# Four more layers of the first block in three passes, and the second block's attention jobs cut in steps behind each layer's gate

## The chip, the core and the metric

One core of a Trainium2 chip. Five engines run side by side and meet only at semaphores: TensorE (PE, with its weight loads PEld), VectorE (DVE), ScalarE (ACT), GpSimd (POOL) and SyncE (SP), whose queue issues all the DMAs here. Each works through its own instructions in the order in which they stand, so an instruction that waits holds everything behind it on that engine. The metric is the time of one execution on the device, in microseconds; less is better.

## What is computed

An attention with decay (a linear recurrence over 768 steps) for 4 sequences and 8 heads of 48, followed by two feed-forward parts on the 3072 tokens of width 384.

```python
for t in range(S):                                   # attention, S = 768
    cur = np.einsum('bhd,bhe->bhde', u[None] * kt, vt)
    y[:, :, t] = np.einsum('bhd,bhde->bhe', rt, state + cur)
    state = wt[:, :, :, None] * state + np.einsum('bhd,bhe->bhde', kt, vt)
...
h = x @ w_in                                         # first part, 384 -> 2048 -> 384
g = h * np.clip(h + 3.0, 0.0, 6.0) / 6.0
x = g @ w_out
...
xn = x / rms * rms_g                                 # second part, 384 -> 1536 -> 384
gate = xn @ w_gate
out = (gate * sigmoid(gate) * (xn @ w_val)) @ w_out
```

## The kernel before

**Blocks, layers, turns.** The tokens go in six blocks of 512 (a chunk of 128 steps of each of the four sequences). For each block the first feed-forward part runs over 16 layers f of 128 hidden columns: `ff1` multiplies the block by the layer's `w_in` into a PSUM tile `hps` (two buffers), ScalarE and VectorE make the gate of it (`emit_act`: a ReLU of `hps` on ScalarE, L455, then a VectorE instruction that takes the minimum and multiplies by `hps`, L456), and `ff2` multiplies the result by the layer's `w_out` into three accumulators `o`. `ff2` of a layer runs two turns after its `ff1`. In the first block the first five layers are taken in two halves of 256 tokens, so that block has 21 turns (0 to 9 are halves; from turn 10 on, turn n is layer n - 5); each later block has 16. Turn 21 is the first of the second block.

**Two ways to multiply.** A layer is done in fp32 (L444, L450: three instructions for `ff1`, three for `ff2`, each of which the profile records as two), or in three fp32r passes of a high part and a low part of both operands (L438, L467: nine instructions each). In the first block the layers below `F32_F` = 12 go in fp32, the four others and all later blocks in three passes. The passes need both operands split. For the weights, `Weight.parts` copies the high part on ScalarE (L161) and subtracts on VectorE (L162). For the block's input, `x_parts` does so for three slices (L594, L595). For the gate's output, `emit_split` copies on ScalarE (L460) and subtracts on GpSimd (L461). Weights come as 64-bit words; `Weight.scale` (ScalarE, L146) and `Weight.bits` (VectorE, L151 and L152) make fp32 of them, and a DMA then writes them to the place where `parts` later reads them.

**Attention jobs.** Each block has four jobs, one for each sequence; jobs 4 to 7 make the second block's input during turns 6 to 20 of the first block, and start at turns n = 6, 9, 12 and 15. A job consists of

- `scans`: two VectorE scans (L273, 128x520) with a reciprocal between them (L281); `bonus1` on GpSimd (L300, L301);
- `muls`: two VectorE multiplications by the scans' results (L296), then `bonus2`, a reduction (L305), and `decay` on GpSimd;
- `fill`: eight ScalarE activations into a tile `a` (L331), which need the reduction's result;
- `pe_a` (L350) and `pe_kt` (L338) on TensorE, which read what `muls` wrote; `choose`: two predicated copies on VectorE into `a` (L356);
- `pe_y` (L386, L392) and `pe_u` (L365) on TensorE, which read `a`; `copy_y` and eight DMAs; then `split` (L414 on ScalarE, L415 on GpSimd) into `xt`, the next block's input.

**What sets the order.** Three lists for each turn n are run around the layer's work: `before[n]`, then `ff1` with its gate, then `between[n]`, then `ff2` of the layer of turn n - 2, then `behind[n]`. `pin` makes the order in which the code emits binding on every engine.

Of the kernel before, what the change touches and what calls it, by code (L numbers as in the profile page):

```python
# [9 lines left out]
F32 = mybir.dt.float32  # L10
# [3 lines left out]
AF = mybir.ActivationFunctionType  # L14
ALU = mybir.AluOpType
AX = mybir.AxisListType

B, H, S, D = 4, 8, 768, 48
# [5 lines left out]
KT = DM // 128  # L24
F1 = 2048 // 128
# [4 lines left out]
WP = 4 * DM  # L30
NG = F2 // 3
LAGS = (5, 0, 0, 0, 0, 0)
F32_F = 12


@with_exitstack
def kernel(
# [15 lines left out]
    nc = tc.nc  # L53
# [23 lines left out]
    x0 = st_p.tile([128, KT, TOK], F32, tag="x0", name="x0", bufs=1)  # L77
# [53 lines left out]

    class Weight:
        def __init__(self, src):
            self.src, self.near = src, False

        def load(self):
            self.raw = st_p.tile([128, 2 * DM], U64, tag="raw", name="raw", bufs=3)
# [11 lines left out]
        def bits(self):  # L149
            x = st_p.tile([128, 2 * DM], U32, tag="x", name="x", bufs=3)  # L150
            nc.vector.tensor_scalar(x, self.words()[0], 29, None, ALU.logical_shift_right)  # L151
            nc.vector.scalar_tensor_tensor(  # L152
                out=x, in0=self.mag.bitcast(U32), scalar=3, in1=x, op0=ALU.logical_shift_left, op1=ALU.bitwise_or)
            self.x = x.bitcast(F32).rearrange("p (a n) -> p a n", a=2)
            nc.sync.dma_start(
                out=self.dst[:, :, 1, :].bitcast(U32), in_=x.rearrange("p (a n) -> p a n", a=2))
            if not self.near:
                self.x = self.dst[:, :, 1, :].bitcast(F32)

        def parts(self):  # L160
            nc.scalar.activation(out=self.dst[:, :, 0, :], in_=self.x, func=AF.Copy)  # L161
            nc.vector.tensor_tensor(  # L162
                out=self.dst[:, :, 1, :], in0=self.x, in1=self.dst[:, :, 0, :].bitcast(F32), op=ALU.subtract)


# [89 lines left out]
    xts = {0: xt_p.tile([128, KT, 2, TOK], F32R, tag="xt", name="xt")}  # L255

    class Job:
# [16 lines left out]
                out=x, data0=x, data1=dd.rearrange("p a h j -> p (a h j)"),  # L274
                initial=0.0, op0=ALU.mult, op1=ALU.add)

        def scans(self):
            nc.vector.memset(dd[:, :, :, 0:1], 1.0)
            self.scan(0)
            self.s1, self.s2 = self.w[:, 0], self.w[:, 1]  # L280
            nc.vector.reciprocal(out=dd[:, :, :, 0:1], in_=self.s1[:, :, :, HF:HF + 1])  # L281
            self.scan(1)

        def decay(self):
            b = self.b
# [172 lines left out]
    def emit_split(a, n, p=None):  # L458
        g = (p or rg_p).tile([128, 2, n], F32R, tag="g", name="g")
        nc.scalar.activation(out=g[:, 0, :], in_=a, func=AF.Copy)  # L460
        nc.gpsimd.tensor_tensor(out=g[:, 1, :], in0=a, in1=g[:, 0, :].bitcast(F32), op=ALU.subtract)  # L461
        return g
# [62 lines left out]
    wa = [Weight(wa_d[f]) for f in range(F1)]  # L525
# [9 lines left out]
    before, between, behind = ([[] for _ in steps] for _ in range(3))  # L535

    def plan(j, n):

        jb = jobs[j]
        before[n] += [jb.scans, jb.bonus1]  # L540
        before[n + 1] += [jb.muls, jb.bonus2, jb.decay]
        before[n + 2] += [jb.fill]
        between[n + 2] += [jb.pe_a, jb.pe_kt, jb.choose, jb.copy_kt]
        between[n + 3] += [jb.pe_y, jb.pe_u, jb.copy_y, jb.add_u]
        if j + 2 < len(jobs):
            behind[n + 3] += [lambda: jobs[j + 2].load("w", "rk", "v")]
        if j + 1 < len(jobs):
            behind[n + 1] += [lambda: jobs[j + 1].load("rks")]
        before[n + 5] += [jb.split]


    j0, j1, j2, j3 = jobs[:B]
# [22 lines left out]
        if f + 3 < F1:  # L575
            behind[n] += [wa[f + 3].load]
    for f in range(F1):
        before[f + 19 if f < F32_F else f + LAGS[0] - 1] += [wa[f].parts]
    behind[2] += [lambda: jobs[4].load("w", "rk", "rks", "v")]
    behind[4] += [lambda: jobs[5].load("w", "rk", "v")]  # L580

# [6 lines left out]
    for c in range(1, NC_):  # L588
        norm_plan(c, first[c], False)

    def x_parts():
        for k in range(KT):
            h = xts[0][:, k, 0, :]
            nc.scalar.activation(out=h, in_=x0[:, k, :], func=AF.Copy)  # L594
            nc.vector.tensor_tensor(out=xts[0][:, k, 1, :], in0=x0[:, k, :], in1=h.bitcast(F32), op=ALU.subtract)  # L595

    behind[F32_F + LAGS[0] - 2] += [x_parts]
    acc, norms, todo = None, {}, []


# [12 lines left out]
    def ff1(c, f, cols):  # L613
        n = cols.stop - cols.start
        ps = ps_h.tile([128, n], F32, tag="h", name="hps")
        if c == 0 and f < F32_F:
            if cols.start:
# [4 lines left out]
        else:  # L622
# [3 lines left out]
            g = emit_split(a, n)  # L626
        x = wa[f].x[:, 1] if c == 0 and f < F32_F else wpair[f][:, 1]
        todo.append((c, f, cols, g, x))

    def ff2(c, f, cols, g, x):  # L630
        nonlocal acc
        first, last = f == 0 and cols.start == 0, f == F1 - 1
        if first:
            acc = new_acc()
        if c == 0 and f < F32_F:
            emit_out_f32(acc, x, g, first, cols)
# [5 lines left out]
    def run(fs):  # L642
        for x in fs:
            x()
# [294 lines left out]
    for i in range(2):  # L939
        nc.sync.dma_start(  # L940
            out=uc[64 * i:64 * i + D, :, i], in_=u_d.rearrange("o (p i d) -> i d (o p)", p=NP, i=2)[i])
# [178 lines left out]
    for j in range(6 * NG + 1):  # L1120
        p, k = divmod(j, 2 * NG)
# [32 lines left out]
        want, n = {4: 7, 5: 7, 6: 6}.get(j, 9), 0  # L1154
# [107 lines left out]
```

## Time and profile before

| | |
|---|---|
| median of 3 runs | 950.96 us (950.94 to 951.01) |
| the profiled execution | 955.21 us, of which its span 953.4 us |
| PE busy | 932.8 us (98%) |
| DVE, POOL, ACT busy | 638.9, 540.5, 476.3 us |
| granted PE clock | 0.996 (mean), of full speed |
| PE share of the chain that ended last | 88% |

The rows below are from the profiled execution, whose times count from the span's start. A busy PE is an engine with instructions under way; the length of a group is best read in the chain of work that ended last, where a group starts when the one before it has ended.

### The profile page before, as it was taken

What the parts mean: (1) busy time and instruction counts of PE and PEld (TensorE: products, weight loads), DVE (VectorE), ACT (ScalarE), POOL (GpSimd) and SP (SyncE); (2) the same over time, 40 slices, a digit from 0 to 9 for tenths busy, and PEclk for the clock granted to TensorE, in tenths of its full rate; (3) what the DMA queues carried; (4) which work ended last, traced back from release to release, by engine and by line L of the source; (5) the groups of instructions that cost most, each with busy time, mean ns of one, the idle gap of its engine ahead of it and who ended that gap; (6) DMA issues with size and microseconds to landing.
All of it is one profiled execution on the core that took longest, in us unless ns stands there. A gap on an engine that the chain in (4) does not pass through costs nothing.

```text
span 953.4 us, 14292 instructions
## 1 busy us (share of the span) xinstructions
PE 932.8 (98%) x5085; PEld 736.3 (77%) x5085; DVE 638.9 (67%) x908; ACT 476.3 (50%) x946; POOL 540.5 (57%) x459
## 2 busy tenths in 40 slices
PE   5899999999999999999999999999999999999998
PEld 5775577778878887777888888787777887888876
DVE  7667776878768787857555386557798557554543
ACT  4544656645654654564454554446545444433331
POOL 0033345766856676774465677579466679235425
PEclk9899999999999999999999999999999999999999
DMA  9686742236654563661662477854699642744321
GB/s 342 237 320 224 279 148 81 84 111 219 208 179 164 174 200 125 219 208 39 236 220 72 152 290 263 290 210 177 203 375 324 260 180 83 248 166 147 151 78 67
DMA packets 63127, 184.77 MB, mean 194 GB/s; under 512 B 8912, under 2 KB 23248, under 8 KB 58448
## 3 DMA queue, kind: packets, MB, share of 16 engines
q1 hardware_dynamic: 63056, 183.87, 54.5%
q8 instruction: 40, 0.66, 0.3%
q14 instruction: 31, 0.25, 0.1%
HBM read 134.29 MB, written 39.32 MB: 182 GB/s over the span
## 4 chain that ended last, share of the span: by engine, by line
PE 88%; DVE 4%; DMA 3%; issue 2%; ACT 2%; POOL 1%; SPq 1%; POOLq 0%; ACTq 0%; DVEq 0%
PE o L467 17%; PE hps L438 16%; PE o L744 14%; PE pe L744 10%; PE pc L744 8%; PE pa L744 4%; PE hps L444 3%; PE o L450 3%; PE pb L744 3%; PE aps L350 2%; PE yps L392 2%; DMA w<-in_dram 2%; PE pd L744 1%; PE ktp L338 1%; PE yps L386 1%
## 5 line engine op out<-in xcount | busy, mean ns | idle before, releaser
L461 POOL TENSOR_TENSOR g<-a,g 128x512 fp32r<-128x512 f32 x84 | 116.5, 1386 | 139.0 <-ACT g L460 138.4
L467 PE MATMUL o<-g,wide_b 128*128 128x512 f32 x441 | 113.4, 399 | 0.0
L456 DVE SCALAR_TENSOR_TENSOR a<-a,hps 128x512 f32<-128x512 f32 x84 | 57.3, 682 | 82.9 <-ACT a L455 82.5
L438 PE MATMUL hps<-xt,wide_b 128*128 128x512 f32 x441 | 111.9, 398 | 0.0
L744 PE MATMUL o<-xt,wide_b 128*128 128x512 f32 x405 | 107.6, 395 | 0.0
L438 PEld LDWEIGHTS hps<-xt,wide_b 128*128 128x128 f32 x441 | 82.7, 187 | 21.2 <-issue 1.0
L455 ACT ACTIVATE a<-hps,half 128x512 f32<-128x512 f32 x84 | 57.3, 682 | 81.0 <-PE hps L438 75.6
L467 PEld LDWEIGHTS o<-g,wide_b 128*128 128x128 f32 x441 | 81.2, 188 | 19.5 <-issue 0.5
L460 ACT ACTIVATE g<-a 128x512 fp32r<-128x512 f32 x84 | 53.1, 633 | 82.3 <-DVE a L456 80.5
L744 PEld LDWEIGHTS o<-xt,wide_b 128*128 128x128 f32 x405 | 75.9, 188 | 18.5 <-ACT planes L234 0.4
L467 PE MATMUL o<-g,wide_a 128*128 128x512 f32 x315 | 78.7, 394 | 0.0
L438 PE MATMUL hps<-xt,wide_a 128*128 128x512 f32 x315 | 77.6, 390 | 0.2 <-POOL xt L415 0.2
L273 DVE TENSOR_TENSOR_SCAN w<-w,dd 128x520 f32<-128x520 f32 x48 | 73.4, 1529 | 4.7 <-DMA w<-in_dram 3.1
L438 PEld LDWEIGHTS hps<-xt,wide_a 128*128 128x128 f32 x315 | 59.0, 188 | 13.3 <-POOL xt L415 0.6
L467 PEld LDWEIGHTS o<-g,wide_a 128*128 128x128 f32 x315 | 58.2, 188 | 12.3 <-issue 0.2
L779 DVE TENSOR_TENSOR q<-pc,q 128x512 f32<-128x512 f32 x80 | 55.0, 688 | 17.8 <-PE pc L744 7.0
L844 POOL TENSOR_TENSOR q<-q,q 128x512 f32<-128x512 f32 x40 | 55.1, 1378 | 14.5 <-DVE q L779 14.3
L331 ACT ACTIVATE a<-iperm,cb 128x128 f32<-128x128 f32 x192 | 58.5, 389 | 0.1
L744 PE MATMUL o<-g,wide_b 128*128 128x512 f32 (+1 forms) x216 | 55.4, 390 | 0.0
L300 POOL TENSOR_TENSOR rks<-rks 128x384 f32<-128x384 f32 x20 | 30.4, 1522 | 43.4 <-DMA rks<-in_dram 38.1
L841 ACT ACTIVATE q<-q 128x512 f32<-128x512 f32 x40 | 25.3, 632 | 51.3 <-DVE q L779 51.3
L844 POOL TENSOR_TENSOR o<-o,o 128x512 f32<-128x512 f32 x10 | 14.1, 1406 | 63.4 <-DVE o L779 63.4
(204 smaller groups left out, 2019.8 us busy)
## 6 DMA issues: line engine op xcount, KB each, us to landing
wraw<-in_dram SPq DMA_DIRECT2D x36, 384.0 KB, 4.1
wide_b<-wo SPq DMA_DIRECT2D x12, 1152.0 KB, 8.0
w<-wd SPq DMA_DIRECT2D x10, 1280.0 KB, 6.0
wide_b<-wd SPq DMA_DIRECT2D x10, 1280.0 KB, 6.0
w<-in_dram SPq DMA_DIRECT2D x24, 520.0 KB, 3.8
rk<-in_dram SPq DMA_DIRECT2D x24, 512.0 KB, 5.0
raw<-in_dram SPq DMA_DIRECT2D x16, 768.0 KB, 7.7
rks<-in_dram SPq DMA_DIRECT2D x20, 384.0 KB, 5.0
```

Source lines behind the costliest of these rows:

```text
L273: nc.vector.tensor_tensor_scan(out=x, data0=x, data1=dd.rearrange("p a h j -> p (a h j)"), initial=0.0, op0=ALU.mult, op1=ALU.add)
L300: nc.gpsimd.tensor_tensor(out=x, in0=x, in1=self.rks[:, 1, :], op=ALU.mult)
L331: nc.scalar.activation(out=self.head(h), in_=iperm, func=AF.Copy, scale=self.cb[:, h, :])
L438: nc.tensor.matmul(ps, slot[:, l, k * 128:(k + 1) * 128], xt[:, k, r, :], start=(k == 0 and j == 0), stop=(k == KT - 1 and j == 2))
L455: nc.scalar.activation(out=a, in_=ps, func=AF.Relu, scale=1.0 / 6.0, bias=half)
L456: nc.vector.scalar_tensor_tensor(out=a, in0=a, scalar=1.0, in1=ps, op0=ALU.min, op1=ALU.mult)
L460: nc.scalar.activation(out=g[:, 0, :], in_=a, func=AF.Copy)
L461: nc.gpsimd.tensor_tensor(out=g[:, 1, :], in0=a, in1=g[:, 0, :].bitcast(F32), op=ALU.subtract)
L467: nc.tensor.matmul(acc[m][:, cols], slot[:, l, m * 128:(m + 1) * 128], g[:, r, :], start=(first and j == 0), stop=(parts or last and j == ...
L744: nc.tensor.matmul(ps, lhs[:, l, :], rhs[:, r, :], start=first and j == 0, stop=True, skip_group_check=not (first and j == 0))
L779: nc.vector.tensor_tensor(out=out, in0=a, in1=b, op=op)
L844: eng.tensor_tensor(out=o, in0=src, in1=self.gate.o[i], op=ALU.mult)
```

## The change

`F32_F` goes from 12 to 8: layers 8 to 11 of the first block now also go in three passes. Their weights' `parts` move from turns 27 to 30 to turns 12 to 15. Weights of layers 8 to 15 are split from the tile in which `bits` made them (`stays`), without the DMA to their place and back. `x_parts` stood whole behind turn 15; it now takes a slice in each of turns 8, 9 and 10, with its subtraction on GpSimd in place of VectorE (`LOW_POOL` is empty: weights are still subtracted on VectorE).

In jobs 4 to 7 the steps stand elsewhere: the first scan behind the gate of turn n, the second behind the gate of turn n + 1, `muls` and `bonus2` behind that (before, both scans stood ahead of the gate of turn n, and `muls` ahead of the gate of turn n + 1), `fill` behind the gate of turn n + 2 in place of ahead of it. `split` of the first three jobs of every block stands behind its turn in place of ahead of it.

```diff
-F32_F = 12
+F32_F = 8
+LOW_POOL = ()
...
             self.x = x.bitcast(F32).rearrange("p (a n) -> p a n", a=2)
+            if self.stays:
+                return
             nc.sync.dma_start(
...
-        def parts(self):
+        def parts(self, pool=False):
             nc.scalar.activation(out=self.dst[:, :, 0, :], in_=self.x, func=AF.Copy)
-            nc.vector.tensor_tensor(
+            (nc.gpsimd if pool else nc.vector).tensor_tensor(
                 out=self.dst[:, :, 1, :], in0=self.x, in1=self.dst[:, :, 0, :].bitcast(F32), op=ALU.subtract)
...
-        def scans(self):
+        def scan_a(self):
             nc.vector.memset(dd[:, :, :, 0:1], 1.0)
             self.scan(0)
             self.s1, self.s2 = self.w[:, 0], self.w[:, 1]
+
+        def scan_b(self):
             nc.vector.reciprocal(out=dd[:, :, :, 0:1], in_=self.s1[:, :, :, HF:HF + 1])
             self.scan(1)
...
         jb = jobs[j]
-        before[n] += [jb.scans, jb.bonus1]
-        before[n + 1] += [jb.muls, jb.bonus2, jb.decay]
-        before[n + 2] += [jb.fill]
-        between[n + 2] += [jb.pe_a, jb.pe_kt, jb.choose, jb.copy_kt]
+        if jb.c == 1:
+            between[n] += [jb.scan_a, jb.bonus1]
+            between[n + 1] += [jb.scan_b, jb.decay]
+            behind[n + 1] += [jb.muls, jb.bonus2]
+            between[n + 2] += [jb.fill, jb.pe_a, jb.pe_kt, jb.copy_kt]
+            behind[n + 2] += [jb.choose]
+        else:
+            before[n] += [jb.scans, jb.bonus1]
+            before[n + 1] += [jb.muls, jb.bonus2, jb.decay]
+            before[n + 2] += [jb.fill]
+            between[n + 2] += [jb.pe_a, jb.pe_kt, jb.choose, jb.copy_kt]
         between[n + 3] += [jb.pe_y, jb.pe_u, jb.copy_y, jb.add_u]
...
-        before[n + 5] += [jb.split]
+        (before if jb.b == B - 1 else behind)[n + 5] += [jb.split]
...
-        before[f + 19 if f < F32_F else f + LAGS[0] - 1] += [wa[f].parts]
+        if f < F32_F:
+            before[f + 19] += [wa[f].parts]
+        else:
+            before[f + LAGS[0] - 1].insert(0, lambda f=f: wa[f].parts(f in LOW_POOL))
...
-    def x_parts():
-        for k in range(KT):
...
+    def x_parts(k):
+        h = xts[0][:, k, 0, :]
+        nc.scalar.activation(out=h, in_=x0[:, k, :], func=AF.Copy)
+        nc.gpsimd.tensor_tensor(out=xts[0][:, k, 1, :], in0=x0[:, k, :], in1=h.bitcast(F32), op=ALU.subtract)
+
+    for k in range(KT):
+        behind[F32_F + LAGS[0] - 5 + k] += [lambda k=k: x_parts(k)]
...
+    for f in range(F32_F, F1):
+        wa[f].stays = True
```

**VectorE around the gates of turns 13 and 14** (job 6, n = 12; a gate is the instruction that reads `hps`; `dd` and `w` are the scans' tiles, `x` the weights being made, `wide_b` their parts). Before, from the first scan's setup, over the gate of turn 12 (the L456 in the middle), to the gate of turn 13:

```order
L278 MEMSET dd 128x8
L273 SCALAR_TENSOR_TENSOR w<-w,dd 128x520
L281 RECIPROCAL dd<-w 128x8
L273 SCALAR_TENSOR_TENSOR w<-w,dd 128x520
L456 SCALAR_TENSOR_TENSOR g<-g,hps 128x512
L374 TENSOR_TENSOR st_105<-st_105,ups 128x192
L151 TENSOR_SCALAR x<-raw 128x768
L152 SCALAR_TENSOR_TENSOR x<-mag,x 128x768
L296 TENSOR_TENSOR rk<-rk,w 128x8x64 x2
L305 TENSOR_REDUCE cb<-rks 128x8
L456 SCALAR_TENSOR_TENSOR g<-g,hps 128x512
```

In the kernel now, from the gate of turn 13 to `choose` behind the gate of turn 14:

```order
L465 SCALAR_TENSOR_TENSOR a<-a,hps 128x512
L286 RECIPROCAL dd<-w 128x8
L276 SCALAR_TENSOR_TENSOR w<-w,dd 128x520
L305 TENSOR_TENSOR rk<-rk,w 128x8x64 x2
L314 TENSOR_REDUCE cb<-rks 128x8
L152 TENSOR_SCALAR x<-raw 128x768
L153 SCALAR_TENSOR_TENSOR x<-mag,x 128x768
L165 TENSOR_TENSOR wide_b<-x,wide_b 128x2x384
L465 SCALAR_TENSOR_TENSOR a<-a,hps 128x512
L365 COPY_PREDICATED a<-mask,aps 128x512 x2
```

The second scan stood ahead of the gate of turn 12 and the two multiplications ahead of that of turn 13; now all three stand behind the gate of turn 13, and the weights' subtraction of layer 10 (L165) stands between them and the gate of turn 14.

**ScalarE at turn 14** (`a<-iperm` is `fill`, L340 now and L331 before; `g<-hps` and `a<-hps` are the ReLU, `g<-a` the copy of the gate's output). Before:

```order
L455 ACTIVATE g<-hps,half 128x512
L146 ACTIVATE mag<-raw 128x768
L414 ACTIVATE xt<-x 128x3x128
L331 ACTIVATE a<-iperm,cb 128x128 x8
L455 ACTIVATE g<-hps,half 128x512
L343 ACTIVATE kt<-ktp 128x512
```

Now:

```order
L464 ACTIVATE a<-hps,half 128x512
L469 ACTIVATE g<-a 128x512
L340 ACTIVATE a<-iperm,cb 128x128 x8
L352 ACTIVATE kt<-ktp 128x512
L423 ACTIVATE xt<-x 128x3x128
L164 ACTIVATE wide_b<-x 128x2x384
```

`fill` stood ahead of the turn's ReLU, and now stands behind the ReLU and behind the copy of the gate's output, which waits for VectorE.

**VectorE from the gate of turn 18 to that of turn 19.** Before:

```order
L456 SCALAR_TENSOR_TENSOR a<-a,hps 128x512
L374 TENSOR_TENSOR st_107<-st_107,ups 128x192
L278 MEMSET dd 128x8
L273 SCALAR_TENSOR_TENSOR w<-w,dd 128x520
L281 RECIPROCAL dd<-w 128x8
L273 SCALAR_TENSOR_TENSOR w<-w,dd 128x520
L162 TENSOR_TENSOR wide_a<-wide_a 128x2x384
L162 TENSOR_TENSOR wide_b<-wide_b 128x2x384
L456 SCALAR_TENSOR_TENSOR a<-a,hps 128x512
```

Now:

```order
L465 SCALAR_TENSOR_TENSOR a<-a,hps 128x512
L383 TENSOR_TENSOR st_107<-st_107,ups 128x192
L165 TENSOR_TENSOR wide_b<-x,wide_b 128x2x384
L281 MEMSET dd 128x8
L276 SCALAR_TENSOR_TENSOR w<-w,dd 128x520
L286 RECIPROCAL dd<-w 128x8
L276 SCALAR_TENSOR_TENSOR w<-w,dd 128x520
L165 TENSOR_TENSOR wide_a<-wide_a 128x2x384
L465 SCALAR_TENSOR_TENSOR a<-a,hps 128x512
```

The weights' subtraction of layer 15, which stood behind the scans of the next job, now stands ahead of them.

## Rows read from the trace of the kernel before

**Rows 1.** Part 1 of the page: busy us, share of the span, instructions.
```profile
PE 932.8 (98%) x5085; PEld 736.3 (77%) x5085; DVE 638.9 (67%) x908; ACT 476.3 (50%) x946; POOL 540.5 (57%) x459
```

**Rows 2.** Stretches of the first block: us, then each engine's busy us, clock, DMA share, GB/s.
```profile
core 0: us, PE busy (x) PEld busy (x) DVE busy (x) ACT busy (x) POOL busy (x), PEclk, DMA share, GB/s
58.00:87.00 29.00, 29.00 (x228) 20.90 (x228) 19.85 (x33) 15.57 (x34) 7.16 (x8) 1.00 0.74 261
87.00:115.00 28.00, 28.00 (x129) 14.33 (x128) 20.55 (x32) 15.13 (x33) 10.07 (x11) 1.00 0.71 244
```

**Rows 3.** Waits of PE from 60 to 260 us: total us, times, longest us.
```profile
PE yps L386 <- DVE a L356: 1.2, 2, 0.7
PE hps L438 <- POOL xt L415: 0.2, 1, 0.2
```

**Rows 4.** Chain that ended last, 64 to 142 us: start us, us, what.
```profile
64.11 1.09 PE aps L350 x16
...
75.81 2.58 PE hps L444 x6
...
91.36 2.58 PE o L450 x6
...
113.33 2.09 PE hps L438 x9
...
115.42 1.09 PE aps L350 x16
...
139.26 2.11 PE o L467 x9
```

**Rows 5.** VectorE in order of time: start us, us, engine, line, operation, tiles, count, [idle before].
```profile
62.06 0.42 DVE L456 SCALAR_TENSOR_TENSOR g<-g,hps 128x256 f32<-128x256 f32 x1 [1.30 <-ACT g L455]
...
70.02 0.21 DVE L281 RECIPROCAL dd<-w 128x8 f32<-128x8 f32 x1
70.26 1.24 DVE L273 TENSOR_TENSOR_SCAN w<-w,dd 128x520 f32<-128x520 f32 x1
...
71.99 1.29 DVE L296 TENSOR_TENSOR rk<-rk,w 128x512 f32<-128x512 f32 x2
73.20 0.55 DVE L305 TENSOR_REDUCE cb<-rks 128x8 f32<-128x384 f32 x1
75.27 0.69 DVE L456 SCALAR_TENSOR_TENSOR g<-g,hps 128x512 f32<-128x512 f32 x1 [1.53 <-ACT g L455]
75.88 0.55 DVE L151 TENSOR_SCALAR x<-raw 128x768 uint32<-128x768 uint32 x1
76.46 0.96 DVE L152 SCALAR_TENSOR_TENSOR x<-mag,x 128x768 uint32<-128x768 uint32 x1
...
92.11 0.69 DVE L456 SCALAR_TENSOR_TENSOR g<-g,hps 128x512 f32<-128x512 f32 x1 [0.16 <-ACT g L455]
...
115.80 0.96 DVE L162 TENSOR_TENSOR wide_b<-wide_b 128x768 fp32r<-128x768 f32 x1 [2.13 <-ACT wide_b L161]
...
117.27 1.34 DVE L356 COPY_PREDICATED a<-mask,aps 128x512 f32<-128x512 uint32 x2
```

**Rows 6.** ScalarE in order of time, same columns.
```profile
112.60 2.44 ACT L331 ACTIVATE a<-iperm,cb 128x128 f32<-128x128 f32 x8
...
117.39 0.63 ACT L460 ACTIVATE g<-a 128x512 fp32r<-128x512 f32 x1 [1.05 <-DVE a L456]
...
125.00 0.83 ACT L161 ACTIVATE wide_b<-wide_b 128x768 fp32r<-128x768 f32 x1
```

**Rows 7.** GpSimd in order of time, same columns.
```profile
132.07 1.62 POOL L461 TENSOR_TENSOR g<-a,g 128x512 fp32r<-128x512 f32 x1 [3.02 <-ACT g L460]
133.65 1.74 POOL L415 TENSOR_TENSOR xt<-x,xt 128x384 fp32r<-128x384 f32 x1
...
190.49 1.95 POOL L300 TENSOR_TENSOR rks<-rks 128x384 f32<-128x384 f32 x1
```

**Rows 8.** VectorE in order of time while GpSimd works beside it, same columns.
```profile
189.71 1.91 DVE L273 TENSOR_TENSOR_SCAN w<-w,dd 128x520 f32<-128x520 f32 x1
...
195.69 2.42 DVE L296 TENSOR_TENSOR rk<-rk,w 128x512 f32<-128x512 f32 x2
```

More of the change, by code (lines that the diff above doesn't have):

```diff
@@ L133, in __init__ @@
         def __init__(self, src):
-            self.src, self.near = src, False
+            self.src, self.near, self.stays = src, False, False
         def load(self):
@@ L280, in scans @@
             self.s1, self.s2 = self.w[:, 0], self.w[:, 1]
+        def scan_b(self):
             nc.vector.reciprocal(out=dd[:, :, :, 0:1], in_=self.s1[:, :, :, HF:HF + 1])
             self.scan(1)
+        def scans(self):
+            self.scan_a()
+            self.scan_b()
         def decay(self):
@@ L589 @@
         norm_plan(c, first[c], False)
-    def x_parts():
-        for k in range(KT):
[L593 to L597, printed above, removed]
+    def x_parts(k):
[4 more added lines that the diff above has]
+        behind[F32_F + LAGS[0] - 5 + k] += [lambda k=k: x_parts(k)]
     acc, norms, todo = None, {}, []
```

## Prediction

> **What bounds the kernel now.** I read part 1 of the page first: PE is busy for 932.8 of 953.4 us [rows 1]. Then the stretches of the first block in which the change works: from 58 to 115 us PE is busy without a gap, at the full granted clock, while VectorE works 19.9 of 29 and 20.6 of 28 us [rows 2]. Then the waits of PE: from 60 to 260 us it waited 1.2 us in two places for `choose` (DVE `a`, L356) and 0.2 us for the second block's input (POOL `xt`, L415), and for nothing else [rows 3]. So here the sum of TensorE's own groups is the time. A change can gain by making them shorter, and can win back 1.4 us of waits at most; moving work between the other engines gains nothing more, and loses as soon as TensorE has to wait. Since TensorE works in order, a wait of `pe_a` or `pe_y` also holds the `ff2` and the `ff1` behind it. That is what I look for.
>
> **What the shorter groups give.** A whole layer's `ff1` takes 2.58 us in fp32 and 2.09 in three passes; `ff2` takes 2.58 and 2.11 [rows 4]. Four layers: 4 x (0.49 + 0.47) = 3.8 us. The weights' subtractions of layers 8 to 11 leave turns 27 to 30, where VectorE also serves jobs; the shorter of the two waits for `choose` (1.2 - 0.7 = 0.5 us, rows 3) stands there, in turn 30, and I count it as gone. Gain: 4.3 us.
>
> The page "FP8 and Floating Point Precision" of the Trainium skill (TensorE Precision Notes) has fp32 as four passes through the array, by which three passes would cost three quarters. The rows give 0.81, not 0.75. By the page a group would save 0.64 us, the change 5.1 us in place of 3.8, and the forecast would be 1.3 us lower; the rows decide.
>
> **Edits at no cost.** `x_parts` on GpSimd, 7.2 and 10.1 us busy in stretches of 29 and 28 [rows 2], is wanted at turn 13 and made by turn 10; if it were late, turn 13 would wait for what is left of three subtractions. Eight DMAs of weights leave SP's queue, which brings the loads behind them forward; PE waits for no DMA here [rows 3]. The copies and subtractions for layers 8 to 11 and their gate outputs lie on ScalarE and GpSimd, which have room; on VectorE 0.96 us a turn is added [rows 5], which counts in the next part. `split` of three jobs in four moves past one turn's work, with the last job still ahead of it; only the last one is on the edge.
>
> **What the moved steps cost.** Before, both scans and `muls` of a job were done ahead of the gate of turn n + 1. Now the second scan starts behind that gate, and `pe_a` in turn n + 2 needs `muls`. Behind the gate stand the reciprocal, 0.21 us, the scan, 1.24, and `muls`, 1.29 [rows 5]: 2.7 us. With GpSimd at work beside it a scan took 1.91 us and `muls` 2.42 [rows 8], so the same three take up to 4.5. I set that against what TensorE has to do meanwhile.
>
> Job 4 (turns 7 and 8, halves): the gate of turn 7 ends at 62.06 + 0.42 = 62.48 [rows 5], so `muls` end at 65.2; TensorE reaches `pe_a` at 64.11 [rows 4]. It waits 1.1 us. Little stands on GpSimd there, so I take no contention.
>
> Job 5 (turns 10 and 11): the gate ends at 75.96 [rows 5], `muls` at 78.7 to 80.5; `pe_a` can start at 75.81 + 2.58 = 78.39 [rows 4]. It waits 0.3 to 2.1 us.
>
> Job 6 (turns 13 to 15). `ff1` of turn 13 ends at 91.36 (where the chain's `ff2` begins, rows 4), its gate at 92.80 [rows 5], 1.44 us later. `muls` end at 95.5 to 97.3. After them `choose` of turn 14 still needs: reduction 0.55, `bits` 0.55 and 0.96, weights' subtraction 0.96, the gate 0.69 [rows 5], then on ScalarE the copy of the gate's output, 0.63, and `fill`, 2.44 [rows 6], which now stands behind that copy, then `choose` itself, 1.34 [rows 5]. Sum 8.1: `choose` ends at 103.7 to 105.5. TensorE: `ff2` 2.58, `ff1` 2.09, `pe_a` and `pe_kt` 1.67 (from 113.33 + 2.09 = 115.42 to the next `ff2` at 117.09, of which 1.09 is `pe_a`; rows 4), `ff2` 2.58, `ff1` 2.09: it reaches `pe_y` at 102.4. It waits 1.3 to 3.1 us in all, part of it at `pe_a`.
>
> Job 7 (turns 16 to 18): the same chain, 1.44 + 2.7 to 4.5 + 8.1 = 12.3 to 14.1 us after the end of `ff1`, but all of TensorE's groups are in three passes now: 2.11 + 2.09 + 1.67 + 2.11 + 2.09 = 10.1. It waits 2.2 to 4.0 us. Here the shorter groups themselves take away what hid the chain.
>
> Sum over the four jobs: 4.9 to 10.3 us. Rows in order of time overlap by up to 0.1 us, which speaks for less, and GpSimd has more to do in these turns than before (`x_parts`, the gates' subtractions of four layers), which speaks for more: I take the middle, 7.6 us.
>
> **The block's edge.** Between the gates of turns 18 and 19 VectorE now has the weights' subtraction of layer 15 ahead of the scans, and that needs ScalarE's copy, which stands behind the copy of the gate's output: 0.63 + 0.83 us [rows 6] in which VectorE did scans before and now stands. The gate of turn 19 comes about 1.5 us later, and on GpSimd the subtraction of that gate's output stands ahead of the last `split` [rows 7], for which the first `ff1` of the second block already waits 0.2 us [rows 3]. Cost 1.5 us; from nothing, if the copy comes early, to 3.3, if scan and copies also run against GpSimd (the same 1.8 us as above).
>
> Sum: 7.6 + 1.5 - 4.3 = **+4.8 us**, with ends of 4.9 + 0 - 4.3 = +0.6 and 10.3 + 3.3 - 4.3 = +9.3. All later groups of TensorE just start later, since it never waits long enough to give this back. The profiled execution would go from 955.21 (span 953.4 and 1.8 around it) to 960.0; that run lies 4.3 us above the median, and I put the difference on the median: 950.96 + 4.8 = **955.8 us**.
>
> **Rivals.**
>
> A, the waits stay at their lower ends and the edge costs nothing: +0.6, 951.6 us. For it: VectorE still idles about 30% of these stretches [rows 2]. Against it: the order on GpSimd puts its work beside `muls` and scans.
>
> B, VectorE falls behind from job to job, since each late gate makes the next one late: the upper ends, +9.3, 960.3 us. For it: a scan goes from 1.24 to 1.91 and `muls` from 1.29 to 2.42 beside a GpSimd instruction that itself takes 1.95 us [rows 5, 7, 8]. The Trainium skill's page "SBUF — State Buffer" (Who interferes with whom) goes further: a VectorE instruction with two SBUF inputs and a GpSimd instruction that reads SBUF do not share, the second one stands until the first is done. The rows fit that for `muls`, not quite for the scan.
>
> C, the other side: the waits are hidden and the gain stands, -4.3, 946.7 us. Place: `pe_a` of jobs 4 to 7. It comes so if VectorE reaches the gates of turns n + 1 so much earlier (no scans ahead of them) that `muls` end in time; it decides where the four waits together stay under 4.3 us. Against it: those gates were not late before. The one of turn 13 had VectorE standing 0.16 us ahead of it, that of turn 10 1.53 us [rows 5], so they come with the ReLU of `hps` and cannot come earlier.
>
> That the change does not do what it says is no case: the order on PE has nine instructions for the four layers.
>
> **How the numbers follow.** Forecast (about +2 to +8) 0.60, A 0.18, B 0.13, C 0.09. The likeliest is the forecast, 955.8. The range leaves out C, A's lower part and B's upper part: 951.0 to 960.0. A difference under 0.2% (1.9 us, 949.1 to 952.9) is about what a measurement of this kernel cannot tell from no change. Faster 0.09 (C), same 0.16 (most of A), slower 0.75.
>
> **What would show it.** Right: waits of PE `aps` for DVE `rk` in turns 8, 11, 14, 17, and of `yps` for DVE `a` in turns 15 and 18, some 7 us together; `ff1` and `ff2` of layers 8 to 11 at 2.1 us a group; a wait of `hps` for POOL `xt` above 1 us at the block's edge. Wrong: if `aps` does not wait for `rk`, `muls` came in time and C holds; if the waits are there but PE's time shrinks elsewhere by more than 4.3 us, I have missed a stretch in which PE was slow without a wait.

## The result

The changed kernel takes 959.58 us (median of 6 runs, 957.87 to 965.54), the kernel before beside it 951.21 us (950.94 to 952.82, 6 runs). The ratio is 1.0081 with a 95% interval of 1.0063 to 1.0099: **slower by 7.7 us (6.0 to 9.4)**, by the ratio; the two medians are 8.4 us apart. The prediction said +4.8, with ends of +0.6 and +9.3. The profiled execution took 961.01 us, its span 959.2 us, 5.8 more than the span before.

Part 1 of the page, after (busy us, share of the span, instructions), answers [rows 1]:

```profile
PE 930.7 (97%) x5109; PEld 742.0 (77%) x5109; DVE 636.1 (66%) x905; ACT 478.1 (50%) x950; POOL 549.2 (57%) x466
```

PE is busy 2.1 us less in a span that is 5.8 us longer. The time was lost in waiting, and some 1.7 us of it to a lower clock behind a wait, not in added work. The same two stretches as in [rows 2] (us, busy us of each engine, clock, DMA share, GB/s):

```profile
58.00:87.00 29.00, 26.72 (x199) 19.10 (x197) 23.14 (x34) 17.38 (x37) 12.41 (x13) 1.00 0.67 233
87.00:115.00 28.00, 26.41 (x174) 18.47 (x171) 22.75 (x31) 14.97 (x28) 12.57 (x12) 1.00 0.43 153
```

Before, PE had no gap here; now it stands 3.9 us in these 57. The waits of PE from 55 to 270 us (total us, times, longest), in place of [rows 3]:

```profile
PE yps L395 <- DVE a L365: 2.6, 2, 1.6
PE hps L447 <- POOL xt L424: 2.4, 1, 2.4
PE aps L359 <- issue: 1.5, 1, 1.5
PE aps L359 <- ACT g L464: 1.3, 1, 1.3
PE aps L359 <- DVE rk L305: 1.0, 1, 1.0
PE aps L359 <- PE hps L447: 0.5, 1, 0.5
```

All four `aps` waits are for the same thing, `muls`, which end 0.06 to 0.11 us ahead of each of these groups. Only the first bears their name (`DVE rk L305`); in the others the view puts the wait down to another event. The rows in order of time (start us, us, engine, line, operation, tiles, count, [idle before]) show where they stand: `pe_a` of jobs 4 to 7, `pe_y` of jobs 6 and 7, and the first `ff1` of the second block.

```profile
64.84 1.16 PE L359 MATMUL aps<-rk 48*128 48x128 f32 x16 [1.01 <-DVE rk L305]
...
80.47 1.16 PE L359 MATMUL aps<-rk 48*128 48x128 f32 x16 [1.28 <-ACT g L464]
...
98.21 1.16 PE L359 MATMUL aps<-rk 48*128 48x128 f32 x16 [0.50 <-PE hps L447]
...
105.73 0.67 PE L395 MATMUL yps<-rk,st 64*64 64x128 f32 x16 [1.09 <-DVE a L365]
...
117.95 1.16 PE L359 MATMUL aps<-rk 48*128 48x128 f32 x16 [1.48 <-issue]
...
125.46 0.67 PE L395 MATMUL yps<-rk,st 64*64 64x128 f32 x16 [1.56 <-DVE a L365]
...
141.17 3.62 PE L447 MATMUL hps<-xt,wide_a 128*128 128x512 f32 x8 [2.43 <-POOL xt L424]
```

The six waits of the jobs are 6.92 us, and the edge is 2.43. The groups did get shorter, and both waits for `choose` in the second block are gone. PE in turns 16 and 17, where no wait stands between the groups:

```profile
110.01 2.26 PE L447 MATMUL hps<-xt,wide_b 128*128 128x512 f32 x9
112.10 2.26 PE L476 MATMUL o<-g,wide_b 128*128 128x512 f32 x9
114.21 2.26 PE L447 MATMUL hps<-xt,wide_b 128*128 128x512 f32 x9
```

Records of neighbouring groups overlap, so their starts count: `ff1` of layer 11 takes 2.09 us, `ff2` of layer 9 2.11, where a layer in fp32 took 2.58 for each [rows 4].

**VectorE, jobs 4 and 6** (same columns as [rows 5]). First the multiplications of job 4, then job 6 from the gate of turn 13 to `choose` of turn 14:

```profile
63.52 1.26 DVE L305 TENSOR_TENSOR rk<-rk,w 128x512 f32<-128x512 f32 x2
...
93.79 0.69 DVE L465 SCALAR_TENSOR_TENSOR a<-a,hps 128x512 f32<-128x512 f32 x1 [1.11 <-ACT a L464]
94.39 0.20 DVE L286 RECIPROCAL dd<-w 128x8 f32<-128x8 f32 x1
94.62 1.24 DVE L276 TENSOR_TENSOR_SCAN w<-w,dd 128x520 f32<-128x520 f32 x1
95.78 2.33 DVE L305 TENSOR_TENSOR rk<-rk,w 128x512 f32<-128x512 f32 x2
98.03 0.54 DVE L314 TENSOR_REDUCE cb<-rks 128x8 f32<-128x384 f32 x1
...
99.95 0.95 DVE L165 TENSOR_TENSOR wide_b<-x,wide_b 128x768 fp32r<-128x768 f32 x1
100.82 0.68 DVE L465 SCALAR_TENSOR_TENSOR a<-a,hps 128x512 f32<-128x512 f32 x1
104.25 1.34 DVE L365 COPY_PREDICATED a<-mask,aps 128x512 f32<-128x512 uint32 x2 [2.74 <-ACT a L340]
```

**GpSimd beside them**, and **ScalarE between the gate and `choose`**:

```profile
95.22 1.75 POOL L470 TENSOR_TENSOR g<-a,g 128x512 fp32r<-128x512 f32 x1 [6.14 <-ACT g L469]
96.91 0.66 POOL L297 TENSOR_TENSOR g<-f,w 128x4 f32<-128x4 f32 x1
```

```profile
101.53 0.63 ACT L469 ACTIVATE g<-a 128x512 fp32r<-128x512 f32 x1 [3.10 <-DVE a L465]
102.07 2.44 ACT L340 ACTIVATE a<-iperm,cb 128x128 f32<-128x128 f32 x8
```

The `muls` of job 4 take 1.26 us, those of job 6 2.33, in the very time in which GpSimd has its subtraction for layer 8 (95.22 to 96.97) and `decay`. Then the gate of turn 14 comes late, `fill` runs behind the copy of the gate's output, and VectorE stands 2.74 us for it ahead of `choose`.

**The edge**, VectorE and then GpSimd:

```profile
128.82 0.34 DVE L383 TENSOR_TENSOR st<-st,ups 128x192 f32<-128x192 f32 x1
130.82 0.96 DVE L165 TENSOR_TENSOR wide_b<-x,wide_b 128x768 fp32r<-128x768 f32 x1 [1.66 <-ACT wide_b L164]
...
131.84 1.92 DVE L276 TENSOR_TENSOR_SCAN w<-w,dd 128x520 f32<-128x520 f32 x1
...
134.03 1.63 DVE L276 TENSOR_TENSOR_SCAN w<-w,dd 128x520 f32<-128x520 f32 x1
...
136.43 0.67 DVE L465 SCALAR_TENSOR_TENSOR a<-a,hps 128x512 f32<-128x512 f32 x1
```

```profile
137.85 1.60 POOL L470 TENSOR_TENSOR g<-a,g 128x512 fp32r<-128x512 f32 x1 [3.29 <-ACT g L469]
139.41 1.71 POOL L424 TENSOR_TENSOR xt<-x,xt 128x384 fp32r<-128x384 f32 x1
```

For comparison VectorE before, at the same place:

```profile
123.96 0.35 DVE L374 TENSOR_TENSOR st<-st,ups 128x192 f32<-128x192 f32 x1 [0.75 <-PE ups L365]
...
128.15 1.71 DVE L162 TENSOR_TENSOR wide_a<-wide_a 128x768 fp32r<-128x768 f32 x1
...
130.66 0.67 DVE L456 SCALAR_TENSOR_TENSOR a<-a,hps 128x512 f32<-128x512 f32 x1
```

VectorE now stands 1.66 us for ScalarE's copy of layer 15, the scans follow, the gate ends at 137.10, and `ff1` starts when the last `split` ends, 4 us later. From the end of `add_u` (L374 before, L383 now) to the gate it is 6.4 us before and 7.3 now. Behind that wait stands something I had not counted. Stretches of 2 us (columns as in [rows 2]; the clock is the third number from the end):

```profile
138.00:140.00 2.00, 0.74 (x3) 0.19 (x1) 1.82 (x3) 1.49 (x3) 2.00 (x2) 1.00 0.98 392
140.00:142.00 2.00, 0.83 (x2) 0.73 (x3) 0.86 (x2) 1.11 (x3) 1.92 (x5) 0.76 1.01 377
142.00:144.00 2.00, 2.00 (x6) 1.52 (x6) 0.00 (x0) 2.00 (x8) 1.23 (x1) 0.50 0.94 350
144.00:146.00 2.00, 2.00 (x21) 1.40 (x20) 1.35 (x2) 1.28 (x2) 0.00 (x0) 0.88 0.63 249
```

The granted clock is 0.50 (1.2 in place of 2.4 GHz) for 3.4 us in all, and the eight instructions that start at 141.17 take 3.6 us, where a whole group of nine takes 2.1.

### The profile page after: what moved, and what is told of

It is laid out like the page before. It is cut to its first block, busy times and chain, and to the rows that moved or that the text cites. A ratio compares the mean times of both kernels' runs of the same rounds, so it can differ in the third digit from the quotient of the medians.

```text
span 959.2 us, 14329 instructions
## 1 busy us (share of the span) xinstructions
PE 930.7 (97%) x5109; PEld 742.0 (77%) x5109; DVE 636.1 (66%) x905; ACT 478.1 (50%) x950; POOL 549.2 (57%) x466
## 4 chain that ended last, share of the span: by engine, by line
PE 88%; DVE 4%; DMA 2%; issue 2%; SPq 1%; ACT 1%; POOL 1%; DVEq 0%; ACTq 0%; POOLq 0%
PE o L476 18%; PE hps L447 18%; PE o L763 14%; PE pe L763 10%; PE pc L763 8%; PE pa L763 4%; PE pb L763 3%; PE aps L359 2%; PE yps L401 2%; PE hps L453 2%; PE o L459 2%; PE pd L763 1%; PE yps L395 1%; PE ktp L347 1%; PE ups L374 1%
## 5 line engine op out<-in xcount | busy, mean ns | idle before, releaser
L470 POOL TENSOR_TENSOR g<-a,g 128x512 fp32r<-128x512 f32 x88 | 122.0, 1387 | 154.5 <-ACT g L469 153.1
L465 DVE SCALAR_TENSOR_TENSOR a<-a,hps 128x512 f32<-128x512 f32 x88 | 60.0, 681 | 95.4 <-ACT a L464 94.0
L476 PE MATMUL o<-g,wide_b 128*128 128x512 f32 x477 | 122.7, 400 | 0.0
L447 PE MATMUL hps<-xt,wide_b 128*128 128x512 f32 x477 | 121.0, 398 | 0.0
L464 ACT ACTIVATE a<-hps,half 128x512 f32<-128x512 f32 x88 | 60.2, 684 | 100.1 <-PE hps L447 95.7
L763 PE MATMUL o<-xt,wide_b 128*128 128x512 f32 x405 | 107.5, 395 | 0.0
L447 PEld LDWEIGHTS hps<-xt,wide_b 128*128 128x128 f32 x477 | 89.5, 188 | 22.8 <-issue 1.4
L476 PEld LDWEIGHTS o<-g,wide_b 128*128 128x128 f32 x477 | 87.7, 188 | 20.9 <-issue 0.5
L469 ACT ACTIVATE g<-a 128x512 fp32r<-128x512 f32 x88 | 55.7, 632 | 90.4 <-DVE a L465 88.2
L763 PEld LDWEIGHTS o<-xt,wide_b 128*128 128x128 f32 x405 | 76.0, 188 | 18.2
L340 ACT ACTIVATE a<-iperm,cb 128x128 f32<-128x128 f32 x192 | 58.5, 388 | 2.0 <-DVE cb L314 1.9
L763 PE MATMUL o<-g,wide_b 128*128 128x512 f32 (+1 forms) x216 | 55.4, 390 | 0.0
L798 DVE TENSOR_TENSOR q<-pe,q 128x512 f32<-128x512 f32 x40 | 27.5, 687 | 30.1 <-PE pe L763 30.1
```

The lines of the kernel that those rows point to most:

```text
L340: nc.scalar.activation(out=self.head(h), in_=iperm, func=AF.Copy, scale=self.cb[:, h, :])
L447: nc.tensor.matmul(ps, slot[:, l, k * 128:(k + 1) * 128], xt[:, k, r, :], start=(k == 0 and j == 0), stop=(k == KT - 1 and j == 2))
L464: nc.scalar.activation(out=a, in_=ps, func=AF.Relu, scale=1.0 / 6.0, bias=half)
L465: nc.vector.scalar_tensor_tensor(out=a, in0=a, scalar=1.0, in1=ps, op0=ALU.min, op1=ALU.mult)
L476: nc.tensor.matmul(acc[m][:, cols], slot[:, l, m * 128:(m + 1) * 128], g[:, r, :], start=(first and j == 0), stop=(parts or last and j == ...
L763: nc.tensor.matmul(ps, lhs[:, l, :], rhs[:, r, :], start=first and j == 0, stop=True, skip_group_check=not (first and j == 0))
```

## The experiments

Theory 1: the waits come from where the change put the steps of the jobs. Theory 2: the passes of four more layers ask more of VectorE than the shorter TensorE groups cover, in whatever order. Theory 3, formed after the first four runs: much of VectorE's lateness is sharing with GpSimd. Differences in us are the ratio to the runs of the kernel before beside it, with the interval in brackets.

**The passes without the new order of the jobs.**

```diff
         if jb.c == 1:
-            between[n] += [jb.scan_a, jb.bonus1]
-            between[n + 1] += [jb.scan_b, jb.decay]
-            behind[n + 1] += [jb.muls, jb.bonus2]
-            between[n + 2] += [jb.fill, jb.pe_a, jb.pe_kt, jb.copy_kt]
-            behind[n + 2] += [jb.choose]
+            before[n] += [jb.scans, jb.bonus1]
+            before[n + 1] += [jb.muls, jb.bonus2, jb.decay]
+            before[n + 2] += [jb.fill]
+            between[n + 2] += [jb.pe_a, jb.pe_kt, jb.choose, jb.copy_kt]
```

> The changed kernel with the steps of jobs 4 to 7 put back in the order of before (scans, muls and fill ahead of the gates), all else as changed: layers 8 to 11 in three passes, x_parts on GpSimd, weights split from where they were made. Theory 1 (order): the waits come from where the steps of the jobs stand. The four waits of pe_a (4.3 us in the changed kernel) and the two of pe_y (2.6 us) go; 3.8 us of shorter groups stay: 947 to 949 us, with what is left of the wait at the block's edge. Theory 2 (VectorE has too much to do): from turn 12 to 20 VectorE has gates, weights, subtractions and jobs to do that take longer than TensorE's shortened groups, in whatever order. Then the waits go over to other places (ff1 for its weights' parts, pe_y), some 5 us of them, and the time is 953 to 957 us.

Measured: 958.24 us, ratio 1.0064, **+6.1 us** (4.3 to 8.0), 1.2 us above the upper end that theory 2 gave. As the only cause theory 1 falls. No `aps` waits are left, but PE in order of time shows others in their place:

```profile
110.39 0.73 PE L447 MATMUL hps<-xt,wide_b 128*128 128x512 f32 x2 [1.80 <-ACT wide_b L164]
111.38 1.90 PE L447 MATMUL hps<-xt,wide_b 128*128 128x512 f32 x7 [0.26 <-DVE wide_b L165]
120.85 0.67 PE L395 MATMUL yps<-rk,st 64*64 64x128 f32 x16 [1.69 <-DVE a L365]
134.43 0.50 PE L447 MATMUL hps<-xt,wide_a 128*128 128x512 f32 x1 [0.75 <-ACT xt L423]
137.31 3.61 PE L447 MATMUL hps<-xt,wide_a 128*128 128x512 f32 x8 [2.37 <-POOL xt L424]
```

6.9 us of waits: for the weights of layer 12, for `choose` of job 7, for the edge; and the last row's 3.61 us says that the clock fell again.

**The new order without the passes** (`F32_F = 12`).

```diff
-F32_F = 8
+F32_F = 12
```

> The changed kernel with F32_F put back to 12: the jobs' steps in their new order, layers 8 to 11 in fp32. Theory 1: the waits of pe_a stay for jobs 4 and 5 (1.0 and 1.3 us); those of jobs 6 and 7 shrink by the 0.5 and 1.0 us that fp32 groups hide more (some 1.5 us left of 4.6), the edge stays at 2 to 4: 955 to 958 us. Theory 2: VectorE is spared four subtractions in turns 12 to 15, jobs 6 and 7 wait for nothing, jobs 4 and 5 still 2.3 us: 953 to 955 us.

Measured: 957.29 us, ratio 1.0041, **+3.9 us** (2.5 to 5.2). Waits: 1.01 and 0.26 for `muls`, 0.65 for `choose`, 2.18 at the edge, 0.91 in the second block, 5.0 in all. The time lies where theory 1 put it, above theory 2's 953 to 955: the order costs without the passes too, at both places that the prediction named. So both parts of the change cost. The two halves alone cost 3.9 and 6.1, together 7.7 and not 10. Each half has the wait at the edge (2.18 and 2.37), and the whole change has it once (2.43), which would account for the difference; the intervals alone would not show one.

**Both scans in one turn, `muls` ahead of the gate of turn n + 1.**

```diff
-            between[n] += [jb.scan_a, jb.bonus1]
-            between[n + 1] += [jb.scan_b, jb.decay]
-            behind[n + 1] += [jb.muls, jb.bonus2]
+            between[n] += [jb.scans, jb.bonus1]
+            before[n + 1] += [jb.muls, jb.bonus2, jb.decay]
```

> The changed kernel with both scans behind the gate of turn n and muls, reduction and decay ahead of the gate of turn n + 1; fill and choose stay where the change put them. Theory 1: the waits of pe_a (4.3 us) go, those of pe_y (2.6) and the edge stay: 955 us. Theory 2: the gates come later by what stands ahead of them now, and what pe_a no longer waits comes back at pe_y, at the weights' parts and at the edge: 957 to 960 us.

Measured: 956.90 us, ratio 1.0036, **+3.4 us** (2.2 to 4.6), between what the two theories gave. The `aps` waits shrink to 0.17, as the prediction's account of job 4 to 7 wants, but `pe_y` of job 7 waits 2.89 (1.56 in the changed kernel), and the clock fell behind that wait, not at the edge (1.17). Of 4.3 us of waits for `muls`, 1.4 came back one step later, as waits for `choose`.

```profile
121.05 0.67 PE L395 MATMUL yps<-rk,st 64*64 64x128 f32 x16 [2.89 <-DVE a L365]
```

**The edge in its old order** (layer 15's `parts` behind the scans).

```diff
-            before[f + LAGS[0] - 1].insert(0, lambda f=f: wa[f].parts(f in LOW_POOL))
+            q = before[f + LAGS[0] - 1]
+            q.insert(len(q) if f == 15 else 0, lambda f=f: wa[f].parts(f in LOW_POOL))
```

> The changed kernel with one thing put back: the weights' subtraction of layer 15 behind the scans of turn 19, as before the change. If the wait of the second block's first ff1 (2.4 us) came from that place, as the prediction says, it goes down to about 1 us, and with it the fall of the granted clock behind it (a first ff1 of 3.6 us in place of 2.1): 956 to 957.5 us. If it comes from VectorE's being late by then anyway, it stays above 2 us and the time stays at 959 us.

Measured: 958.72 us, ratio 1.0059, **+5.6 us** (3.7 to 7.6), above what I expected. The wait for `xt` went from 2.43 to 0.42 and no clock fell, but turn 20 now waits 1.43 for layer 15's weights (`wide_b`). So the wait at the edge does come from this place, as the prediction says. But undoing it gives only some 2 us of the 7.7 back, with intervals that overlap.

**Without the new GpSimd work.** The low parts of the first block's input and of the gates of layers 8 to 12 are not made.

```diff
-        nc.gpsimd.tensor_tensor(out=g[:, 1, :], in0=a, in1=g[:, 0, :].bitcast(F32), op=ALU.subtract)
+        if low:
+            nc.gpsimd.tensor_tensor(out=g[:, 1, :], in0=a, in1=g[:, 0, :].bitcast(F32), op=ALU.subtract)
...
-        nc.gpsimd.tensor_tensor(out=xts[0][:, k, 1, :], in0=x0[:, k, :], in1=h.bitcast(F32), op=ALU.subtract)
...
-            g = emit_split(a, n)
+            g = emit_split(a, n, low=int(c > 0 or f > 12))
```

> The changed kernel without the GpSimd subtractions that the change adds beside the jobs: the low part of the first block's input and of the gates of layers 8 to 12 is not made, TensorE reads the high part in its place, in as many instructions (so part of the computation is left out). Theory 3 (VectorE's lateness comes to a large part from sharing with GpSimd): both multiplications of muls take 1.3 us in jobs 5 to 7, as in job 4, in place of 2.3, TensorE's waits for rk and a fall from 6.9 to 3 to 4.5 us, and the time is 2.5 to 4 us below that of the changed kernel (about 956). Theory 2 (too much work on VectorE, whoever works beside it): muls get shorter or not, the waits go down by less than 1 us, and the time stays within 1 us of the changed kernel's (about 959).

Measured: 956.98 us, ratio 1.0046, **+4.4 us** (3.0 to 5.7), some 3 us under the changed kernel. `muls` of jobs 5 and 6 on VectorE:

```profile
75.78 1.27 DVE L305 TENSOR_TENSOR rk<-rk,w 128x512 f32<-128x512 f32 x2
...
92.47 1.27 DVE L305 TENSOR_TENSOR rk<-rk,w 128x512 f32<-128x512 f32 x2
```

2.29 and 2.33 became 1.27, as did the 2.32 of job 7, and the jobs' waits fell from 6.92 to 3.91. Theory 3 holds for 3 us: with nothing else changed on VectorE, taking away what GpSimd does beside it gave that back. The edge (2.43, and the clock) and VectorE's stand of 2.75 us for `fill` stayed.

The Trainium skill's page "SBUF — State Buffer" (Who interferes with whom) says that a VectorE instruction with two SBUF inputs contends with a GpSimd instruction that reads SBUF, one standing until the other is done. Here the multiplications agree (1.27 alone, 2.3 with a subtraction of 1.75 us beside them, behind whose end they end 1.1 us later). For the scan the addition is smaller: 1.24 alone, 1.92 at 131.84.

**The weights' subtractions on GpSimd** (old order of the jobs, layer 15's `parts` in its old place).

```diff
-LOW_POOL = ()
+LOW_POOL = (8, 9, 10, 11, 12, 13, 14)
```

> Three passes from layer 8 on with the jobs in the order of before; the weights' subtractions of layers 8 to 14 on GpSimd in place of VectorE, that of layer 15 in its place of before. Theory 2: VectorE has some 7 x 0.95 us less to do in turns 12 to 18, the waits of turns 17 and 18 (1.8 + 0.3 + 1.7 us in the run of the three passes alone) go, and with them most of its loss: 950 to 954 us. Theory 3: seven more subtractions of 1.8 to 1.9 us on GpSimd stand beside scans and multiplications, which then take 1.9 and 2.3 us more often; VectorE wins nothing, GpSimd is late for the splits, and the time stays at 956 to 960 us.

Measured: 954.29 us, ratio 1.0020, **+1.9 us** (0.9 to 3.0). With the passes alone it was +6.1. Most of the loss goes, near what theory 2 gave and far from theory 3's 956 to 960, although GpSimd is busy 22.6 of the 28 us from 87 to 115. But two things differ from the passes alone, the engine of the subtractions and the place of layer 15's `parts`, and the next run has the same time with all the subtractions on VectorE: what GpSimd gives by itself is not shown. What is left are 3.2 us of waits for layer 12's weights in turn 17, and the clock's fall behind them.

**All `parts` behind their turn's scans** (old order of the jobs).

```diff
-            before[f + LAGS[0] - 1].insert(0, lambda f=f: wa[f].parts(f in LOW_POOL))
+            q = before[f + LAGS[0] - 1]
+            q.insert(len(q), lambda f=f: wa[f].parts(f in LOW_POOL))
```

> Four layers in three passes, the jobs as before, and the weights' subtractions behind the scans and multiplications of their turn in place of ahead of them: nothing of the order of before is touched but what the passes need. Theory 1: the gain of 3.8 us stands but for a wait of 1 to 1.5 us at turn 20 (as in the run with the old order at the edge): 948 to 950. Theory 2: the waits only change their names (wide_b at turns 17 and 20 in place of xt at 21), 3 to 6 us above before: 954.5 to 958.

Measured: 954.85 us, ratio 1.0021, **+2.0 us** (1.0 to 3.0): the time is at the lower end of theory 2's, the loss under its 3 to 6 us. The waits changed their names as theory 2 says (2.25 at turn 16 and 2.17 at turn 20, both for `wide_b`), but no clock fell. Within the old order this place is some 4 us better than the front, so theory 2's "in whatever order" does not hold: the place of the passes' own subtractions counts too.

**Two layers in place of four** (as the kernel just told, `F32_F = 10`).

```diff
-F32_F = 8
+F32_F = 10
```

> Only layers 10 and 11 change to three passes (F32_F = 10), the jobs and the place of the weights' subtractions as in the kernel before. The shorter groups of two layers give 1.9 us, the wait in turn 30 that goes up to 0.5. Theory 2 (each shorter group takes cover from work that VectorE cannot do sooner): waits of 1.5 to 4 us come from turn 17 on, and the time is that of before, within 2 us (950 to 953 on a chip where before takes 951 to 952). Theory 1 (the places of the change cost, not the passes): no new wait, 947 to 949.5.

Measured: 952.02 us, ratio 0.9996, **-0.4 us** (-2.1 to +1.4). Two waits are left, 0.86 at turn 20 and 0.41 at the edge. That is not to be told from no change. By the waits (1.3 us here, 5.0 with four layers in the kernel just told) half the layers cost far less than half: the waits grow faster than the gain.

**`fill` back ahead of the gate**, the rest as changed.

```diff
-            between[n + 2] += [jb.fill, jb.pe_a, jb.pe_kt, jb.copy_kt]
-            behind[n + 2] += [jb.choose]
+            before[n + 2] += [jb.fill]
+            between[n + 2] += [jb.pe_a, jb.pe_kt, jb.choose, jb.copy_kt]
```

> The changed kernel with fill back ahead of the gate of turn n + 2 and choose behind pe_kt, as before; scans and muls stay in two steps behind the gates. The step of the prediction under test: the waits of pe_y in turns 15 and 18 (1.09 and 1.56 us in the changed kernel) come from fill standing behind the copy of the gate's output. If so, those two waits go (VectorE's stand of 2.7 us for a ahead of choose goes with them), the waits of pe_a for rk stay (1.0 to 2.3 us a job, up to 1 us longer where TensorE now comes earlier), the edge stays at 2.4 with the clock's fall behind it, and the time is 0.5 to 2.5 us below the changed kernel's: 956.5 to 959 where before takes 951 to 952.5. If instead VectorE as a whole is late (theory 2), the waits of yps go over to aps in full and the time stays within 0.5 us of the changed kernel's.

Measured: 961.33 us, ratio 1.0088, **+8.4 us** (6.5 to 10.4). As to the step, the prediction is right: both waits of `pe_y` in turns 15 and 18 go, and so does VectorE's stand ahead of `choose`. As to the time, I was wrong: it isn't shown to be lower. `pe_y` of job 4 now waits 0.76, the edge 0.47 and 2.38. The waits of the profiled execution are 8.1 us in place of 9.4; the interval of the time overlaps with that of the changed kernel. The mean granted clock of these runs is 0.993, that of the kernel before in the same comparison 0.997: estimated from these two some 4 us of clock lost, where one fall is 1.7.

**Three layers, subtractions on GpSimd** (jobs in the old order, layer 15's `parts` behind the scans).

```diff
-F32_F = 8
-LOW_POOL = ()
+F32_F = 9
+LOW_POOL = (8, 9, 10, 11, 12, 13, 14)
```

> Layers 9 to 11 in three passes (F32_F = 9), jobs in the order of before, weights' subtractions of layers 9 to 14 on GpSimd, that of layer 15 in its place of before. If the runs of parts_on_gpsimd (waits of 3.2 us at turn 17 left) and two_layers (1.3 us of waits in the first block) are read rightly, the fourth layer is what takes the last cover away and VectorE's subtractions are the rest: three layers give 2.9 us and the waits of block two 1.2, new waits stay under 1.5 us in all, and the time is 2 to 4 us below before (948 to 950.5 where before takes 952). If GpSimd's subtractions cost as much as they spare (they stand beside scans and muls): within 1 us of before.

Measured: 950.54 us (12 runs), before beside it 952.76 (17 runs), ratio 0.9966, **-3.2 us** (-5.0 to -1.6). It beats both kernels. The waits of PE that are left from 55 to 270 us:

```profile
PE hps L447 <- DVE wide_b L165: 0.9, 1, 0.9
PE hps L447 <- POOL xt L424: 0.4, 1, 0.4
```

**The sum for all.** New waits less the 1.4 us of before, plus 1.7 us for each fall of the clock behind 55 us in the profile, less 0.95 us for each layer:

| kernel | layers | waits, us | falls | sum | measured |
|---|---|---|---|---|---|
| the change | 4 | 9.4 | 1 | +5.9 | +7.7 |
| passes alone | 4 | 6.9 | 1 | +3.4 | +6.1 |
| order alone | 0 | 5.0 | 0 | +3.6 | +3.9 |
| `muls` early | 4 | 5.4 | 1 | +1.9 | +3.4 |
| old edge | 4 | 8.8 | 0 | +3.6 | +5.6 |
| no low parts | 4 | 6.3 | 1 | +2.8 | +4.4 |
| subtractions on GpSimd | 4 | 3.7 | 1 | +0.2 | +1.9 |
| `parts` behind | 4 | 5.0 | 0 | -0.2 | +2.0 |
| two layers | 2 | 1.3 | 0 | -2.0 | -0.4 |
| `fill` early | 4 | 8.1 | 1 | +4.6 | +8.4 |
| three layers | 3 | 1.3 | 0 | -3.0 | -3.2 |

The order of the kernels comes out nearly right. The kernels with four layers measure 1.5 to 2.7 us above their sum, `fill` early 3.8, two layers 1.6. The traces say where this does not lie. Take TensorE's first wait for `st` behind 40 us (at 46.20 before, L338, L347 now) and its first wait for `q` in the second part (604.61 before, L744, L763 now). Between these two the profiled executions differ from that of before by +6.1, +3.9, +3.8, +2.3, +4.2, +3.1, +0.9, +0.9, -1.9, +4.9 and -2.9 us, in the order of the table: the sum with 0.1 to 0.7 us on top, 1.1 for `parts` behind. From there to the end they differ by 0.3 us at most. So the rest is either ahead of 46 us, a place that the twelve profiles reach at 42.7 to 46.8 us, or in executions of which no profile was kept. Part of it could be falls of the clock in the timed runs: the runs of the passes alone have a mean clock of 0.995, those of before 0.998. But `parts` behind has the clock of before, and the 2 us all the same. What they are stays open.

## Why the prediction was right, and where it was off

The sign and its mechanism were right: the change shortens what TensorE does and makes it wait longer than it saves, at the six places in the jobs and the one at the edge that the prediction named. The number is less good than the range makes it look: 959.58 lies 0.4 us under the range's upper end. The terms as measured in the profile give the table's +5.9 in place of +4.8, since an edge that was 2.4 us too cheap stands against jobs and a second block that were 0.7 us each too dear, which is luck; what lies between +5.9 and the measured +7.7 no run explains. Step by step:

- **Shorter groups**, 3.8: the two groups of layer 8 to 11 have the length that the rows gave. **Waits gone in the second block**: both (1.2 us, [rows 3]), not one (0.5). With the order alone the later one stays (0.91), so the passes take it away, as the prediction says; the other shrinks there to 0.15, by something else in the change that no run singles out.
- **Jobs**, 7.6 (4.9 to 10.3): measured 6.9. Job 4 1.01 (1.1), job 5 1.28 (0.3 to 2.1), job 6 0.50 + 1.09 (1.3 to 3.1), job 7 1.48 + 1.56 (2.2 to 4.0). Each lies inside its bounds. The choice of no contention for job 4 (1.26 us) and some for the others (2.3) was right, and the run without the low parts shows it for jobs 5 to 7. But that run also shows that one edit listed at no cost had one: the third slice of `x_parts` on GpSimd (1.77 us from 77.45) stands beside `muls` of job 5, whose wait is 1.28 with it and 0.25 without it.
- **The edge**, 1.5 (0 to 3.3): the wait grew by 2.2, and the fall of the clock behind it added some 1.7, together 3.9, outside the bounds. This is the step that failed in size. The stand for ScalarE's copy was foreseen (1.46 us, measured 1.66), and it made the gate 0.9 us later against `add_u`. But `add_u` itself came some 1.5 us later against TensorE: it ends 2.9 us ahead of the end of turn 19's `ff1`, before 4.4. VectorE had only ended `choose` of job 7 at 125.3 us and stood nowhere from there to `add_u`. The two `ff1`, now and before:

```profile
129.75 2.26 PE L447 MATMUL hps<-xt,wide_b 128*128 128x512 f32 x9
```

```profile
126.05 2.66 PE L438 MATMUL hps<-xt,wide_b 128*128 128x512 f32 x9
```

  That is rival B's mechanism, lateness handed on, and the edge is where it was paid. And I had treated a wait of PE as costing its own length, which the clock proved wrong.
- **Rival B** (9.3 us in all) came nearer to the measured 7.7 than rival A, but not by its own account: the jobs' waits stayed at their middle, not their upper ends.
- **Rival C** needed `muls` in time. The run with `muls` early has them in time and is 3.4 us slower than before, not 4.3 faster: beyond its condition C lacked the next ones, `choose` and the edge, which take the wait over.
- **The median.** The prediction put the difference on the median, the profiled execution of before being 4.3 us above it. That is not borne out: the profiled executions differ by 5.8 us, near the sum of the terms, the timed runs by 7.7. The changed kernel's profile lies 1.4 us above its median, and it starts as slowly as that of before (both have a mean clock of 0.83 from 20 to 40 us; with three layers it is 0.91). So the start of the two profiles does not tell them apart, and why the timed runs lie further apart stays open.

## What to carry to other kernels

Where the engine that bounds is full, every microsecond taken from it is also cover taken from the engines that feed it: sum up, for each turn, what the feeding engine must do between two of its hand-overs, and shorten the bound only as far as that fits (three layers here, not four). A wait removed by a new order tends to come back under another name one hand-over later, so undo parts of a change one at a time before believing a wait's label. And when work is put on GpSimd, ask which two-input instruction of VectorE will run beside it, and whether that one is on the path.

## What the runs showed of the hardware

- **A wait of 2 to 3 us can cost some 1.7 us more than its length.** The granted clock fell to 0.5 for 3.4 us within 1.5 us of the end of a wait of PE in the profiles of the change (2.43), of the passes alone (0.75 and 2.37), of no low parts (2.43), of `muls` early (2.89), of `fill` early (0.47 and 2.38), and of the subtractions on GpSimd (2.08 and 1.17); not behind 2.18 (order alone), 2.25 and 2.17 (`parts` behind) or 1.43 (old edge). Each fall is some 1.7 us. That the wait brings on the fall is read from this order of events; why 2.43 has one and 2.25 none no run shows. The Trainium skill's page "TensorE: Matmul & The Clock Gate" (HAM oscillation — how this bites in real kernels) tells of a kernel whose waits for transfers let the clock fall again and again. Here too the falls stand behind waits, though for other engines' results, and behind 55 us no profile has more than one.
- **`muls` of 128x512 with two inputs from SBUF take 1.27 us alone and 2.3 beside a GpSimd subtraction**, a scan of 128x520 1.24 and up to 1.92, and GpSimd's own subtraction of 128x512 goes from 1.30 (at 102.25 in the changed kernel) to 1.75. Both sides get slower, which makes work on GpSimd dearer than its own rows say.
